# Second half of K in two 256-column banks, a new order of the queries, and memory reciprocals kept in PSUM

## The chip, the cores and the metric

The kernel runs on one core of a Trainium2 chip. The metric is the device time in microseconds (us) of one execution. The core has five engines with a queue each: TensorE (PE, with its weight loads shown apart as PEld), VectorE (DVE), ScalarE (ACT), GpSimd (POOL) and SyncE (SP, which here only issues DMAs). Matmuls write PSUM, eight banks of 512 fp32 columns; ScalarE and VectorE read it from there.

## The reference

Two things are computed from `x` (2048 rows of 512) and mixed by a gate. The part that matters is an attention that runs over 64 segments of 32 rows, one after the other, and hands eight memory rows from each to the next:

```python
for s in range(n_seg):                       # 64 segments of 32 rows
    h = jnp.concatenate([mem, xs], axis=1)   # 8 memory rows + 32 rows
    q, k, v = h @ Wq, h @ Wk, h @ Wv         # 32 heads of 128
    scores = jnp.einsum('bhqe,bhke->bhqk', q, k) * scale
    scores = jnp.where(mask[None, None], scores, -1000000000.0)
    p = _softmax(scores, axis=-1)
    o = jnp.einsum('bhqk,bhke->bhqe', p, v)
    o = jnp.einsum('bhte,hed->btd', o, Wo)
    mem = o[:, :M, :].copy()                 # the next segment needs this
    outs.append(o[:, M:, :])
...
return g * a + (1 - g) * b                   # a: attention, b: an MLP on x
```

The mask lets the eight memory queries see all keys and the others only earlier ones.

## The kernel before

It has three stages: the MLP (`b`) and the gate for all rows, the loop over the 64 segments, and a tail for the last segment. The order of the work on each engine is written out by hand; nothing is moved by a scheduler. Each engine takes its instructions in the order written, and waits are put in where data or buffers ask for them.

**How a segment is cut.** Of the 40 rows of a segment, 32 go through the step-by-step path: the eight memory rows and the first 24 others ("ride", `RIDE`). The last eight rows ("left", `LEFT`) don't hang on the memory, so their Q, K and V are made for four segments at once, ahead of time, as side work (`left_qk`, `left_v`), and so is their output projection (`wo_left`), behind time. The generator `fill` deals the side work out in units of four matmuls of 512 columns; `run(W1)`, `run(W2)` and `run(W3)` put two units each at three places of the segment, and what is left goes at the end.

**Order of a segment** (the `for s` loop; lines as in the profile):

1. Projections (`qk_unit`, L110): Q and K, each in two halves of 16 heads, into the four banks `U[0]` to `U[3]`, in the order Q0, K0, Q1, K1. A half is 16 matmuls of 512 columns: four chunks of the contraction, times four tiles of 32 array columns that run side by side. After each half ScalarE casts the bank to `Tb` (`qk_cast`, L115) and VectorE transposes it in 32x32 blocks into `QT` or `KT` (`qk_tr`, L119). After Q0 stand the four matmuls that write the mask into the second score bank (`mask_mm(1)`, L248).
2. First scores (`scores(s, 0)`, L256 and L260): heads 0 to 15 into bank `SbF`, on top of the mask, then two exps (L674): memory queries, then the rest.
3. V (`v_unit`, L129): the first half into bank `X1` (four groups), its cast (L689); one group of the second half into `X2`; the sums for the memory queries of the first heads (`msum(0)`, L267 and L270) and their normalising (`mnorm(0)`: reciprocal to `R`, L681, and multiply into `E`, L682); one more V group.
4. Second scores (`scores(s, 1)`): heads 16 to 31 into bank `W`, two exps, and a copy of the left queries' part of `E` into a zero-padded tile `EZ` (L699); the last two V groups and the cast of V's second half (L702); `msum(1)` and `mnorm(1)`.
5. `run(W1)`; the sums of the other queries (`xsums`, L605) and their reciprocal (`recip_x`, L616), which goes through DRAM to be spread over all partitions (`r_dr`, `Rb`, on SP); GpSimd adds the reciprocals to a running check (`racc`, L621).
6. Attention times V (`av`, L280 and L285): heads 0 to 15, then 16 to 31, into `U`; it needs both V casts and the normalised `E`.
7. ScalarE copies the memory columns to `UT` (L712) and the others to `XR` (`x_raw`, L611); `run(W2)`; output projection into `W` (`wo_pass`, L141), cast to `w` (L635); the mask for the first score bank; `run(W3)`; in every fourth segment the finished 128 rows of output are put together (`out_sel`, L226 and L228).
8. Selection of the memory rows (L724) and their cast into the next segment's input `hT` (L725), from which the next projections start.

GpSimd brings the other inputs to `hT` (`prep_h`, L239), the left queries to `QT` (`prep_q`, L243), and multiplies `XR` by `Rb` (`x_norm`, L629) during the next segment. The order of the columns of `QT`, and so of the scores and of `E`, is memory, ride, left. `E` has 56 columns per head: left keys with memory queries (0 to 8), all other keys with the 40 queries (8 to 48), left keys with left queries (48 to 56).

Of the kernel before, what the change touches and what calls it, by code (L numbers as in the profile page):

```python
# [27 lines left out]
def kernel(ctx, tc, A_x, A_mem0, A_Wq, A_Wk, A_Wv, A_Wo, A_seg_len, B_x, B_w1, B_b1, B_w2, B_b2, gate_w, out):  # L28
# [78 lines left out]
    def qk_unit(bk, G, t, hf, kc):  # L107
        h0, h1 = HF[hf]
        for j in range(4):
            nc.tensor.matmul(bk[32 * j:32 * j + 32, :], lhsT=G[:, kc, :], rhs=W5[t][:, kc, h0:h1, j, :],  # L110
                             start=(kc == 0), stop=(kc == KC - 1), tile_position=(0, 32 * j))

    def qk_cast(bk):
        Tb = ew.tile([P, 8, 32, 2], BF16, tag="Tb", bufs=3, name="Tb")
        nc.scalar.copy(out=Tb[:], in_=bk.rearrange("p (a b e) -> p a e b", a=8, b=2))  # L115
        return Tb

    def qk_tr(Tb, dst, hf):
        nc.vector.transpose(out=dst[:, 8 * hf:8 * hf + 8, 0:32, :].rearrange("p a r b -> p a (r b)").bitcast(FP32),  # L119
                            in_=Tb[:].rearrange("p a e b -> p (a e b)").bitcast(FP32))  # L120
# [115 lines left out]

    def prep_h(s):
        T, si = divmod(s, SPT)
        nc.gpsimd.tensor_copy(out=hT[s % 3][:, :, M:32], in_=xTs[T][:, :, seg * si:seg * si + RIDE])  # L239

    def prep_q(s):
        T, si = divmod(s, SPT)
        nc.gpsimd.tensor_copy(out=QT[:, :, 32:40, :].bitcast(FP32),  # L243
                              in_=QL[T % 2][:].bitcast(FP32).rearrange("p a (l s) b -> p a l s b", s=SPT)[:, :, :, si])

# [19 lines left out]
    def sums(out, E, c_main, c_left, n, start):  # L265
        for j in range(4):
            nc.tensor.matmul(out[32 * j:32 * j + 32], lhsT=BO[:, 32 * j:32 * j + 32], rhs=E[:, :, c_main:c_main + n],  # L267
                             start=start, stop=False, skip_group_check=True, tile_position=(0, 32 * j))
        for j in range(4):
            nc.tensor.matmul(out[32 * j:32 * j + 32, :, n - 8:n], lhsT=BO[:, 32 * j:32 * j + 32], rhs=E[:, :, c_left:c_left + 8],  # L270
                             start=False, stop=True, skip_group_check=True, tile_position=(0, 32 * j))
# [20 lines left out]
    with tc.tile_pool(name="mlpw", bufs=1) as mlpw, \  # L292
# [81 lines left out]
        for c in range(4):  # L374
            nc.gpsimd.affine_select(out=SelM[:], in_=SelM[:], pattern=[[-1, M]], compare_op=ALU.not_equal, fill=1.0, base=-32 * c, channel_multiplier=1)
            nc.gpsimd.affine_select(out=SelI[:], in_=SelI[:], pattern=[[-1, 32]], compare_op=ALU.not_equal, fill=1.0, base=-32 * c, channel_multiplier=1)
            nc.gpsimd.affine_select(out=SelR[:, 0:RIDE], in_=SelR[:, 0:RIDE], pattern=[[-1, RIDE]], compare_op=ALU.not_equal, fill=1.0, base=-32 * c - M, channel_multiplier=1)
            nc.gpsimd.affine_select(out=SelL[:].rearrange("p (s t) -> p s t", s=SPT)[:, :, RIDE:seg], in_=SelL[:].rearrange("p (s t) -> p s t", s=SPT)[:, :, RIDE:seg],
                                    pattern=[[-LEFT, SPT], [-1, LEFT]], compare_op=ALU.not_equal, fill=1.0, base=-32 * c, channel_multiplier=1)

        def consts():
            nc.vector.tensor_scalar(out=rr[:, 0:1], in0=ri[:], scalar1=31, scalar2=None, op0=ALU.bitwise_and)
            nc.vector.tensor_scalar(out=rr[:, 2:3], in0=rr[:, 0:1], scalar1=2, scalar2=None, op0=ALU.logical_shift_right)
            nc.vector.tensor_scalar(out=rr[:, 1:2], in0=rr[:, 0:1], scalar1=3, scalar2=None, op0=ALU.bitwise_and)
            nc.vector.tensor_copy(out=rf[:], in_=rr[:])
            nc.vector.tensor_copy(out=iof[:], in_=io[:])
            nc.vector.tensor_scalar(out=rf[:, 0:1], in0=rf[:, 0:1], scalar1=float(M), scalar2=None, op0=ALU.subtract)
            nc.vector.tensor_scalar(out=mk1[:], in0=iof[:, 0:4], scalar1=rf[:, 1:2], scalar2=MASK_NEG, op0=ALU.not_equal, op1=ALU.mult)
            yield
            for a in range(4):  # L390
                nc.vector.tensor_scalar(out=Mk[:, a, 16:16 + RIDE], in0=iof[:], scalar1=rf[:, 0:1], scalar2=MASK_NEG, op0=ALU.is_lt, op1=ALU.mult)
                nc.vector.tensor_copy(out=Mk[:, a, 0:8], in_=mk1[:, a:a + 1].to_broadcast([P, 8]))
                nc.vector.tensor_scalar(out=Mk[:, a, 48:56], in0=iof[:, 0:8], scalar1=rf[:, 2:3], scalar2=MASK_NEG, op0=ALU.is_lt, op1=ALU.mult)
                nc.vector.tensor_scalar(out=Mk[:, a, 48:56], in0=Mk[:, a, 48:56], scalar1=mk1[:, a:a + 1], scalar2=None, op0=ALU.add)
                yield
# [84 lines left out]
        def first():  # L480
# [3 lines left out]
            dve_q.append(lambda: nc.vector.tensor_copy(out=hT[0][:, :, 0:M], in_=m0p))  # L484
# [112 lines left out]
    EZ = [lp.tile([P, NG, 32], BF16, name=f"EZ{i}") for i in range(2)]  # L597
    for i in range(2):
        nc.gpsimd.memset(EZ[i][:, :, 0:RIDE], 0.0)

    def xsums(s, E):
        for first, src, c0 in ((True, E, 16), (False, EZ[s % 2], 0)):
            for i in range(NG):
                c, h = i % 4, i // 4
                nc.tensor.matmul(xs8[32 * c:32 * c + 32, 4 * h:4 * h + 4], lhsT=src[:, i, c0:c0 + 32], rhs=BO[:, 0:P:32],  # L605
                                 start=first and h == 0, stop=not first, skip_group_check=True, tile_position=(0, 32 * c))

    def x_raw(s):
        XR = cw.tile([P, 4, NG, 32], BF16, tag="XR", name="XR")
        for j in range(4):  # L610
            nc.scalar.copy(out=XR[:, j], in_=U[j][:, 0:NG * 40].rearrange("p (i q) -> p i q", q=40)[:, :, 8:40])  # L611
        XRs[s] = XR

    def recip_x(s):
# [5 lines left out]
        nc.sync.dma_start(Rb[:].rearrange("p r e -> p (r e)"), r_dr[s % 2][:].rearrange("r e -> (r e)").partition_broadcast(P))  # L620
        nc.gpsimd.tensor_tensor(out=racc[:, 0:RW], in0=racc[:, 0:RW], in1=R[:, 0:RW], op=ALU.add)  # L621
        Rbs[s] = Rb

    def x_norm(s):
        T, si = divmod(s, SPT)
        XR, Rb = XRs.pop(s), Rbs.pop(s)[:].rearrange("p (c q) (h j) -> p h j c q", c=4, h=2)
        for out, o, a, b in ((UT[(s + 1) % 2], M, 0, RIDE), (UL[T % 2], LEFT * si, RIDE, 32)):
# [10 lines left out]
    W1, W2, W3 = 2, 2, 2  # L638
    for s in range(nseg):
        T, si = divmod(s, SPT)  # L640
        last = s == nseg - 1
        hc, hn = hT[s % 3], hT[(s + 1) % 3]
        fill = side(T, si)
# [13 lines left out]
        for n, (t, hf) in enumerate(((0, 0), (1, 0), (0, 1), (1, 1))):  # L657
# [14 lines left out]
        def exps(i2, x):  # L672
            c = slice(16, EW) if x else slice(0, 16)
            nc.scalar.activation(out=E[:, 4 * i2:4 * i2 + 4, c], in_=Sb[i2][:, :, c], func=ACTF.Exp, scale=scale)  # L674

        def msum(i2):
            sums(U[i2][:, 320:352].rearrange("p (i q) -> p i q", q=8), E[:, 4 * i2:4 * i2 + 4, :], 8, 0, 8, True)
# [27 lines left out]
        msum(1)  # L705
        mnorm(1)
# [4 lines left out]
        for j in (0, 2, 1, 3):  # L711
            nc.scalar.copy(out=UT[s % 2][:, j, :, 0:M], in_=U[j][:, 0:NG * 40].rearrange("p (i q) -> p i q", q=40)[:, :, 0:8])  # L712
# [12 lines left out]
        nc.vector.tensor_copy(out=hn[:, :, 0:M], in_=W[:, 0:KC * M].rearrange("p (k m) -> p k m", k=KC))  # L725
# [8 lines left out]
    sums(xsum, E, 16, 48, 32, True)  # L734
# [6 lines left out]
    nc.vector.tensor_tensor(out=E[:, :, 16:48], in0=E[:, :, 16:48], in1=Rr, op=ALU.mult)  # L741
    nc.vector.tensor_tensor(out=E[:, :, 48:56], in0=E[:, :, 48:56], in1=Rr[:, :, 24:32], op=ALU.mult)
    av(s, V, E)
    UF = UT[(s + 1) % 2]
    for j in (0, 2, 1, 3):
        (nc.scalar.copy if j % 2 == 0 else nc.vector.tensor_copy)(out=UF[:, j], in_=U[j][:, 0:NG * 40].rearrange("p (i q) -> p i q", q=40)[:, :, 8:40])
# [147 lines left out]
```

## Time and profile before

| | us |
|---|---|
| median of 3 runs | 795.08 (794.21 to 796.0) |
| the profiled execution | 796.19 |
| its span, first to last instruction | 794.4 |
| loop over segments starts (first Q projection) | 98.7 |
| a segment, from one first Q projection to the next (median) | 10.65; every fourth 10.85 |
| last segment's first Q projection | 774.5 |
| mean granted TensorE clock | 0.998 |

The loop is 676 us of 794. TensorE is busy 97% of the span, ScalarE 68%, VectorE 41%, GpSimd 35%. The matmuls of a group overlap, so TensorE's 97% does not say that it works at its peak; the waits are to be read from when groups start. In the timeline a row gives start and length in us, engine, line, operation and the tiles written and read; a number in brackets is the idle time of the engine ahead of it and what ended it.

### The profile page before, as it was taken

The numbers are of one execution on the slowest core, as the hardware profiler recorded it, in microseconds if no ns is written. First come the engines' busy times: TensorE is split into PE (matmuls) and PEld (weight loads), VectorE is DVE, ScalarE is ACT, GpSimd is POOL, SyncE is SP. The second block draws the span as 40 slices with busy tenths as digits, with TensorE's granted clock in tenths as the row PEclk, the third lists the DMA queues.
The fourth block names the chain that finished last, engine by engine and source line by source line (L and its number), as shares of the span: only waits on it lengthen the run. The fifth ranks groups of instructions, "written<-read, shape, count | busy, mean of one in ns | idle before, by whom it ended". The sixth has DMA issues, their size and how long they took to land.

```text
span 794.4 us, 42412 instructions
## 1 busy us (share of the span) xinstructions
PE 767.9 (97%) x18921; PEld 428.8 (54%) x18950; DVE 327.7 (41%) x1061; ACT 539.9 (68%) x1503; POOL 277.8 (35%) x519
## 2 busy tenths in 40 slices
PE   7999999999999999999999999999999999999996
PEld 5666555555555555555555555555555555555553
DVE  4776344333334343434343333434343434333334
ACT  3666676766777676767776677777677767776663
POOL 3111033343344434234334324443334434332332
PEclk9999999999999999999999999999999999999999
DMA  6779411212111222211121212122221212121211
GB/s 189 265 269 350 142 59 58 74 60 86 60 53 68 77 70 70 77 57 60 60 86 61 86 61 75 46 75 70 78 70 57 62 58 86 61 80 60 71 65 36
DMA packets 46723, 70.49 MB, mean 89 GB/s; under 512 B 12799, under 2 KB 36456, under 8 KB 45000
## 3 DMA queue, kind: packets, MB, share of 16 engines
q1 hardware_dynamic: 45016, 64.97, 25.0%
q8 instruction: 150, 2.46, 1.3%
q0 software_dynamic: 720, 1.97, 0.7%
q10 hardware_dynamic: 800, 0.79, 0.3%
q14 instruction: 37, 0.30, 0.1%
HBM read 59.06 MB, written 4.45 MB: 80 GB/s over the span
## 4 chain that ended last, share of the span: by engine, by line
PE 93%; ACT 4%; issue 1%; DVE 1%; DMA 1%; POOL 0%; SPq 0%; DVEq 0%; POOLq 0%; ACTq 0%
PE U L110 28%; PE X L129 18%; PE W L141 14%; PE X L110 7%; PE U L468 5%; PE U L280 4%; PE X L141 3%; ACT w L635 3%; PE W L462 3%; PE SbF L462 3%; PE W L724 2%; PE U L267 1%; PE SbF L605 1%; PE SbF L256 1%; PE W L248 1%
## 5 line engine op out<-in xcount | busy, mean ns | idle before, releaser
L629 POOL TENSOR_TENSOR UT<-XR,Rb 128x384 bf16<-128x384 bf16 x126 | 140.0, 1132 | 271.8 <-DMA Rb<-r_dr 211.7
L115 ACT CAST Tb<-U 128x512 bf16<-128x512 f32 x258 | 151.0, 585 | 83.2 <-PE U L110 82.7
L110 PEld LDWEIGHTS <-hT 128*32 128x32 bf16 x4096 | 103.9, 97 | 109.7 <-DVE hT L725 19.1
L110 PE MATMUL U<-Wq_sb,hT 128*32 128x512 bf16 x2048 | 132.8, 379 | 1.1 <-DVE hT L725 1.1
L129 PE MATMUL X<-Wv_sb,hT 128*32 128x512 bf16 x2048 | 133.2, 378 | 0.0
L110 PE MATMUL U<-Wk_sb,hT 128*32 128x512 bf16 x2048 | 132.7, 379 | 0.0
L141 PE MATMUL W<-Wo_sb,UT 128*32 128x512 bf16 x2080 | 124.6, 380 | 1.5 <-ACT UT L712 1.2
L725 DVE CAST hT<-W 128x32 bf16<-128x32 f32 x63 | 12.1, 192 | 231.2 <-PE W L724 231.2
L119 DVE STREAM_TRANSPOSE QT<-Tb 128x256 f32<-128x256 f32 x128 | 57.0, 445 | 82.2 <-ACT Tb L115 81.1
L141 PEld LDWEIGHTS <-UT 128*32 128x32 bf16 x2080 | 57.2, 96 | 58.0 <-POOL racc L621 19.0
L119 DVE STREAM_TRANSPOSE KT<-Tb 128x256 f32<-128x256 f32 x128 | 57.0, 445 | 58.2 <-ACT Tb L115 58.2
L611 ACT CAST XR<-U 128x256 bf16<-128x256 f32 x252 | 78.6, 438 | 0.0
L635 ACT CAST w<-W 128x512 bf16<-128x512 f32 x65 | 38.0, 585 | 45.2 <-PE W L141 45.2
L629 POOL TENSOR_TENSOR UL<-XR,Rb 128x128 bf16<-128x128 bf16 x126 | 60.4, 500 | 0.0
L712 ACT CAST UT<-U 128x64 bf16<-128x64 f32 x252 | 35.3, 227 | 31.3 <-PE U L285 31.3
L129 PEld LDWEIGHTS <-hT 128*32 128x32 bf16 x2048 | 45.2, 95 | 20.7
L681 DVE RECIPROCAL R<-U 128x32 f32<-128x32 f32 x126 | 45.0, 357 | 25.9 <-PE U L270 23.0
L621 POOL TENSOR_TENSOR racc<-racc,R 128x72 f32<-128x72 f32 x63 | 21.2, 336 | 97.9 <-DVE R L616 95.2
L468 PE MATMUL U<-w_sb,hTm 128*128 128x512 bf16 (+1 forms) x163 | 49.5, 381 | 0.6
L115 ACT CAST Tb<-X 128x512 bf16<-128x512 f32 x62 | 36.5, 589 | 16.4 <-PE X L110 16.4
L462 PEld LDWEIGHTS <-w_sb 128*128 128x128 bf16 (+1 forms) x352 | 34.7, 102 | 21.1 <-issue 4.0
L256 PEld LDWEIGHTS <-KT 128*32 128x32 bf16 x2048 | 33.7, 95 | 16.3 <-DVE KT L119 0.2
(158 smaller groups left out, 1176.0 us busy)
## 6 DMA issues: line engine op xcount, KB each, us to landing
Rb<-r_dr SPq DMA_DIRECT2D x63, 512.0 KB, 3.9
Wv_sb<-in_A_Wv_dram SPq DMA_DIRECT2D x4, 1024.0 KB, 7.0
Wq_sb<-in_A_Wq_dram SPq DMA_DIRECT2D x4, 1024.0 KB, 7.2
Wk_sb<-in_A_Wk_dram SPq DMA_DIRECT2D x4, 1024.0 KB, 10.7
Wo_sb<-in_A_Wo_dram SPq DMA_DIRECT2D x4, 1024.0 KB, 14.8
VP<-VL SPq DMA_DIRECT2D x64, 64.0 KB, 3.0
xt<-in_A_x_dram SPq DMA_DIRECT2D x16, 128.0 KB, 2.7
xs<-in_A_x_dram SPq DMA_DIRECT2D x16, 128.0 KB, 2.3
```

The source lines that it names most:

```text
L110: nc.tensor.matmul(bk[32 * j:32 * j + 32, :], lhsT=G[:, kc, :], rhs=W5[t][:, kc, h0:h1, j, :], start=(kc == 0), stop=(kc == KC - 1), tile_ ...
L115: nc.scalar.copy(out=Tb[:], in_=bk.rearrange("p (a b e) -> p a e b", a=8, b=2))
L119: nc.vector.transpose(out=dst[:, 8 * hf:8 * hf + 8, 0:32, :].rearrange("p a r b -> p a (r b)").bitcast(FP32), in_=Tb[:].rearrange("p a e b ...
L129: nc.tensor.matmul(bk[32 * j:32 * j + 32, :], lhsT=G[:, kc, :], rhs=Wv5[:, kc, 4 * vb:4 * vb + 4, j, :], start=(kc == 0), stop=(kc == KC - ...
L141: nc.tensor.matmul(bk[32 * c:32 * c + 32, :], lhsT=U_[:, j, i, :], rhs=Wo_sb[:, 4 * i + j, :], start=(n == 0), stop=(n == NW - 1), tile_po ...
L256: nc.tensor.matmul(Sb[i2][32 * j:32 * j + 32, i - 4 * i2, M:M + 40], lhsT=KT[:, h // 2, :, h % 2], rhs=QT[:, h // 2, :, h % 2], start=Fals ...
L462: nc.tensor.matmul(hp[:rows, 0:TB * P], lhsT=w1_sb[:, kc, fc * P:fc * P + rows], rhs=yTs[blk][:, kc, :], start=(kc == 0), stop=(kc == KC - 1))
L468: nc.tensor.matmul(bp(blk, tt)[:], lhsT=hTm[blk % 2][:rows, fc, tt * P:(tt + 1) * P], rhs=w2_sb[:rows, fc, :], start=(fc == 0), stop=(fc = ...
L611: nc.scalar.copy(out=XR[:, j], in_=U[j][:, 0:NG * 40].rearrange("p (i q) -> p i q", q=40)[:, :, 8:40])
L629: nc.gpsimd.tensor_tensor(out=out[:, :, 4 * h:4 * h + 4, o:o + b - a], in0=XR[:, :, 4 * h:4 * h + 4, a:b], in1=Rb[:, h, :, :, a:b], op=ALU ...
L635: nc.scalar.copy(out=w[:], in_=W[:])
L681: nc.vector.reciprocal(out=r, in_=U[i2][:, 320:352])
```

## The change

1. **Second half of K.** K1 is projected in two quarters of eight heads, 256 columns each: the first into `U[3]`, the second into `X2`. Each has its own cast and its own transpose (`k_tr`). Matmul instructions for K1 go from 16 to 32.
2. **Query order.** Left, ride, memory instead of memory, ride, left, in `hT`, `QT`, `E`, the masks, the selections and the copies out of `U`. Left and ride are then neighbours: `xsums` reads left queries straight from `E`, as eight columns, and the padded tile `EZ` and its copy are gone. In every segment's `E` the columns 0 to 40 are the other queries and 40 to 56 the memory queries.
3. **Order after the first scores.** `mask_mm(1)` stands behind the first scores instead of behind Q0. The first bank's two exps become one of 56 columns per head. The second scores come after three V groups instead of six, both memory sums after the second scores, and V ends behind them (three groups behind the second sums). Both V casts stand behind all exps.
4. **Memory reciprocals in PSUM.** `mnorm` writes its reciprocals to spare columns of the two score banks (`RP`) and multiplies from there; two copies in `recip_x` bring them to `R` later, for the check.
5. **Smaller ones.** `out_sel` does its last matmul, 128 array columns wide, as four tiles of 32. The side work is dealt out 1, 2, 3 instead of 2, 2, 2 in the second and third segment of each four.

```diff
     def qk_unit(bk, G, t, hf, kc):
-        h0, h1 = HF[hf]
+        h0, h1 = hf if isinstance(hf, tuple) else HF[hf]
...
     def qk_cast(bk):
         Tb = ew.tile([P, 8, 32, 2], BF16, tag="Tb", bufs=3, name="Tb")
-        nc.scalar.copy(out=Tb[:], in_=bk.rearrange("p (a b e) -> p a e b", a=8, b=2))
+        n = bk.shape[1] // 64
+        nc.scalar.copy(out=Tb[:, 0:n], in_=bk.rearrange("p (a b e) -> p a e b", a=n, b=2))
         return Tb
+    def k_tr(Tb, a0, n):
+        nc.vector.transpose(out=KT[:, a0:a0 + n].rearrange("p a r b -> p a (r b)").bitcast(FP32),
+                            in_=Tb[:, 0:n].rearrange("p a e b -> p (a e b)").bitcast(FP32))
...
-        nc.tensor.matmul(bk[:], lhsT=SelL[:], rhs=wls.pop(T)[:], start=False, stop=True, skip_group_check=True)
+        wl = wls.pop(T)
+        for si in range(SPT):
+            nc.tensor.matmul(bk[32 * si:32 * si + 32, :], lhsT=SelL[:, 32 * si:32 * si + 32], rhs=wl[:], start=False, stop=True,
+                             skip_group_check=True, tile_position=(0, 32 * si))
...
+    RP = [bk[:, 288:320] for bk in (SbF, W)]
...
-        for first, src, c0 in ((True, E, 16), (False, EZ[s % 2], 0)):
+        for first, c0, n in ((True, 8, 32), (False, 0, LEFT)):
             for i in range(NG):
                 c, h = i % 4, i // 4
-                nc.tensor.matmul(xs8[32 * c:32 * c + 32, 4 * h:4 * h + 4], lhsT=src[:, i, c0:c0 + 32], rhs=BO[:, 0:P:32],
+                nc.tensor.matmul(xs8[32 * c:32 * c + n, 4 * h:4 * h + 4], lhsT=E[:, i, c0:c0 + n], rhs=BO[:, 0:P:32],
...
+        for i2 in (1, 0):
+            nc.vector.tensor_copy(out=R[:, 32 * i2:32 * i2 + 32], in_=RP[i2])
         nc.gpsimd.tensor_tensor(out=racc[:, 0:RW], in0=racc[:, 0:RW], in1=R[:, 0:RW], op=ALU.add)
...
-    W1, W2, W3 = 2, 2, 2
+    WS = ((2, 2, 2), (1, 2, 3), (1, 2, 3), (2, 2, 2))
...
-        for n, (t, hf) in enumerate(((0, 0), (1, 0), (0, 1), (1, 1))):
+        for n, (t, hf) in enumerate(((0, 0), (1, 0), (0, 1))):
...
             if n == 0:
                 flush(act_q, 9)
-                mask_mm(1)
                 flush(dve_q, 9)
-            qk_tr(qk_cast(bk[:]), (QT, KT)[t], hf)
+            qk_tr(qk_cast(bk[:]), (QT, KT)[t], hf, LEFT * (1 - t))
+        for bk, a0 in ((U[3], NP // 2), (X2, 3 * NP // 4)):
+            n = NP // 4
+            bk = bk[:, 0:64 * n]
+            for kc in range(KC):
+                qk_unit(bk, hc, 1, (2 * a0, 2 * a0 + 2 * n), kc)
+            k_tr(qk_cast(bk), a0, n)
...
         def mnorm(i2):
-            r, e = R[:, 32 * i2:32 * i2 + 32], E[:, 4 * i2:4 * i2 + 4, 0:16].rearrange("p i (a q) -> p i a q", q=8)
+            r, e = RP[i2], E[:, 4 * i2:4 * i2 + 4, 40:56].rearrange("p i (a q) -> p i a q", q=8)
...
         scores(s, 0)
-        for i2 in range(2):
-            exps(0, i2)
-        for kc in range(KC):
+        mask_mm(1)
+        nc.scalar.activation(out=E[:, 0:4, :], in_=Sb[0], func=ACTF.Exp, scale=scale)
+        for kc in range(3):
             v_unit(X1, hc, 0, kc)
-        nc.scalar.copy(out=v_out(V, 0), in_=X1[:])
-        v_unit(X2, hc, 1, 0)
-        if not last:
-            msum(0)
-            mnorm(0)
-        v_unit(X2, hc, 1, 1)
         scores(s, 1)
         for i2 in range(2):
             exps(1, i2)
         if not last:
-            nc.scalar.copy(out=EZ[s % 2][:, :, RIDE:32], in_=E[:, :, 48:56])
-        for kc in range(2, KC):
+            msum(0)
+            mnorm(0)
+        v_unit(X1, hc, 0, 3)
+        nc.scalar.copy(out=v_out(V, 0), in_=X1[:])
+        v_unit(X2, hc, 1, 0)
+        if not last:
+            msum(1)
+            mnorm(1)
+        for kc in range(1, KC):
             v_unit(X2, hc, 1, kc)
         nc.scalar.copy(out=v_out(V, 1), in_=X2[:])
         if last:
             break
-        msum(1)
-        mnorm(1)
         run(W1)
```

The rest of the diff renumbers columns and slices for the new query order, in the masks, the selections and the tail.

More of the change, by code (lines that the diff above doesn't have):

```diff
@@ L269, in sums @@
         for j in range(4):
-            nc.tensor.matmul(out[32 * j:32 * j + 32, :, n - 8:n], lhsT=BO[:, 32 * j:32 * j + 32], rhs=E[:, :, c_left:c_left + 8],
+            nc.tensor.matmul(out[32 * j:32 * j + 32, :, 0:8], lhsT=BO[:, 32 * j:32 * j + 32], rhs=E[:, :, c_left:c_left + 8],
                              start=False, stop=True, skip_group_check=True, tile_position=(0, 32 * j))
@@ L375 @@
             nc.gpsimd.affine_select(out=SelM[:], in_=SelM[:], pattern=[[-1, M]], compare_op=ALU.not_equal, fill=1.0, base=-32 * c, channel_multiplier=1)
-            nc.gpsimd.affine_select(out=SelI[:], in_=SelI[:], pattern=[[-1, 32]], compare_op=ALU.not_equal, fill=1.0, base=-32 * c, channel_multiplier=1)
+            for q0, a, b in ((0, RIDE, 32), (LEFT, 0, RIDE)):
+                nc.gpsimd.affine_select(out=SelI[:, a:b], in_=SelI[:, a:b], pattern=[[-1, b - a]], compare_op=ALU.not_equal, fill=1.0, base=-32 * c - q0, channel_multiplier=1)
             nc.gpsimd.affine_select(out=SelR[:, 0:RIDE], in_=SelR[:, 0:RIDE], pattern=[[-1, RIDE]], compare_op=ALU.not_equal, fill=1.0, base=-32 * c - M, channel_multiplier=1)
@@ L483, in first @@
                 nc.tensor.transpose(m0p[:, kc, :], m0[:, kc * P:(kc + 1) * P], ident[:M, :M])
-            dve_q.append(lambda: nc.vector.tensor_copy(out=hT[0][:, :, 0:M], in_=m0p))
+            dve_q.append(lambda: nc.vector.tensor_copy(out=hT[0][:, :, RIDE:32], in_=m0p))
             yield from x_mm(0, X2)
@@ L610, in x_raw @@
         for j in range(4):
-            nc.scalar.copy(out=XR[:, j], in_=U[j][:, 0:NG * 40].rearrange("p (i q) -> p i q", q=40)[:, :, 8:40])
+            nc.scalar.copy(out=XR[:, j], in_=U[j][:, 0:NG * 40].rearrange("p (i q) -> p i q", q=40)[:, :, 0:32])
         XRs[s] = XR
@@ L626, in x_norm @@
         XR, Rb = XRs.pop(s), Rbs.pop(s)[:].rearrange("p (c q) (h j) -> p h j c q", c=4, h=2)
-        for out, o, a, b in ((UT[(s + 1) % 2], M, 0, RIDE), (UL[T % 2], LEFT * si, RIDE, 32)):
+        for out, o, a, b in ((UT[(s + 1) % 2], M, LEFT, 32), (UL[T % 2], LEFT * si, 0, LEFT)):
             for h in range(2):
@@ L642 @@
         hc, hn = hT[s % 3], hT[(s + 1) % 3]
+        W1, W2, W3 = WS[si]
         fill = side(T, si)
@@ L711 @@
         for j in (0, 2, 1, 3):
-            nc.scalar.copy(out=UT[s % 2][:, j, :, 0:M], in_=U[j][:, 0:NG * 40].rearrange("p (i q) -> p i q", q=40)[:, :, 0:8])
+            nc.scalar.copy(out=UT[s % 2][:, j, :, 0:M], in_=U[j][:, 0:NG * 40].rearrange("p (i q) -> p i q", q=40)[:, :, 32:40])
         x_raw(s)
@@ L724 @@
             nc.tensor.matmul(W[:, M * k:M * k + M], lhsT=w[:, k * P:(k + 1) * P], rhs=SelM[:], start=(k == 0), stop=(k == KC - 1), skip_group_check=True)
-        nc.vector.tensor_copy(out=hn[:, :, 0:M], in_=W[:, 0:KC * M].rearrange("p (k m) -> p k m", k=KC))
+        nc.vector.tensor_copy(out=hn[:, :, RIDE:32], in_=W[:, 0:KC * M].rearrange("p (k m) -> p k m", k=KC))
         flush(dve_q, 9)
@@ L733 @@
     nx = slice(8 * NG, 40 * NG)
-    sums(xsum, E, 16, 48, 32, True)
+    sums(xsum, E, 8, 0, 32, True)
     for _ in out_sel(T - 1, X2):
@@ L740 @@
     Rr = R[:, nx].rearrange("p (i q) -> p i q", q=32)
-    nc.vector.tensor_tensor(out=E[:, :, 16:48], in0=E[:, :, 16:48], in1=Rr, op=ALU.mult)
-    nc.vector.tensor_tensor(out=E[:, :, 48:56], in0=E[:, :, 48:56], in1=Rr[:, :, 24:32], op=ALU.mult)
+    nc.vector.tensor_tensor(out=E[:, :, 8:40], in0=E[:, :, 8:40], in1=Rr, op=ALU.mult)
+    nc.vector.tensor_tensor(out=E[:, :, 0:8], in0=E[:, :, 0:8], in1=Rr[:, :, 0:8], op=ALU.mult)
     av(s, V, E)
@@ L745 @@
     for j in (0, 2, 1, 3):
-        (nc.scalar.copy if j % 2 == 0 else nc.vector.tensor_copy)(out=UF[:, j], in_=U[j][:, 0:NG * 40].rearrange("p (i q) -> p i q", q=40)[:, :, 8:40])
+        (nc.scalar.copy if j % 2 == 0 else nc.vector.tensor_copy)(out=UF[:, j], in_=U[j][:, 0:NG * 40].rearrange("p (i q) -> p i q", q=40)[:, :, 0:32])
     flush(dve_q, 9)
```

24 lines of the change are left out of this document (11 added, 13 removed).

## The prediction

> **What bounds the kernel now.** I read the page's busy times first, then the timeline of one segment, then that of a segment near the end that has no side work, and last the groups of instructions with their shapes kept apart.
>
> ```profile
> span 794.4 us, 42412 instructions
> ...
> PE 767.9 (97%) x18921; PEld 428.8 (54%) x18950; DVE 327.7 (41%) x1061; ACT 539.9 (68%) x1503; POOL 277.8 (35%) x519
> ```
>
> TensorE looks full, but that row counts overlapping matmuls. The segment that starts near 399.4 us shows what its stretches wait for (columns: start, length, engine, line, operation, what ended the idle time).
>
> ```profile
> 402.99 0.27 PE L256 MATMUL SbF<-QT,KT 128*32 128x40 bf16 x16
> ...
> 403.12 1.25 PE L129 MATMUL X<-Wv_sb,hT 128*32 128x512 bf16 x20
> ...
> 403.21 0.58 ACT L115 CAST Tb<-U 128x512 bf16<-128x512 f32 x1 [0.28 <-PE U L110]
> ...
> 403.83 0.45 DVE L119 STREAM_TRANSPOSE KT<-Tb 128x256 f32<-128x256 f32 x1 [0.42 <-ACT Tb L115]
> ...
> 404.47 0.27 PE L256 MATMUL W<-QT,KT 128*32 128x40 bf16 x16
> ...
> 404.60 0.61 PE L129 MATMUL X<-Wv_sb,hT 128*32 128x512 bf16 x8
> 404.82 0.10 PEld L267 LDWEIGHTS <-BO 128*32 128x32 bf16 x1
> 404.86 0.42 ACT L674 ACTIVATE E<-W 128x64 bf16<-128x64 f32 x2
> ...
> 405.13 0.20 PE L267 MATMUL U<-E,BO 128*32 128x32 bf16 x4
> ...
> 405.46 0.58 ACT L702 CAST V<-X 128x512 bf16<-128x512 f32 x1
> ...
> 405.88 0.23 DVE L682 TENSOR_TENSOR E<-E,R 128x64 bf16<-128x64 bf16 x1
> ...
> 406.15 0.28 PE L280 MATMUL U<-E,V 32*128 32x40 bf16 x16
> ...
> 406.87 1.91 PE L141 MATMUL W<-Wo_sb,UT 128*32 128x512 bf16 x32
> ```
>
> The reader should see: the last K matmuls end shortly after 402.99; their cast and transpose end at 404.28, just before the second scores at 404.47. The second sums (405.13) come 0.53 after those scores end (404.60), though only 0.43 of V work lies between. The second half of attention times V (406.15) starts 0.05 after the multiply on VectorE ends (405.88 + 0.23). So from the second scores on it is a chain of hand-overs that sets the time, and the side work fills its holes. The proof is a segment that has no side work:
>
> ```profile
> 762.36 0.28 PE L248 MATMUL SbF<-Mk,ident 128*32 128x224 bf16 x4
> 762.59 0.58 ACT L635 CAST w<-W 128x512 bf16<-128x512 f32 x1 [0.65 <-PE W L141]
> 763.23 0.26 PE L724 MATMUL W<-SelM,w 128*128 128x8 bf16 x4 [0.59 <-ACT w L635]
> ```
>
> Its first projections start at 753.17 and the next segment's at 763.84, 10.67 apart; a segment with eight units of side work takes 10.70 (410.29 to 420.99). A fill that is moved is therefore worth nothing as long as it ends inside the wait it fills. The rows also price one hand-over: from the end of the output projection's issue (762.36) over a 512-wide cast to the next matmul (763.23) it is 0.87.
>
> **The change part by part**, counted from the start of the first scores (0 = 402.99), per segment; there are 63 whole ones.
>
> *Ahead of the scores.* The mask matmuls of the second score bank leave the projections: four matmuls take 0.095 (411.16 to 411.25, next group's start). The second half of K becomes 32 matmuls of 256 columns. A group of four 512-wide ones takes 0.216 (20 matmuls, five groups, 403.12 to 404.20), the 224-wide mask group 0.095, so a 256-wide group takes 0.108 and eight take 0.87, against 0.86: +0.01. Together -0.085.
>
> *Up to the second scores.* First scores 0.13, mask 0.095, three V groups 0.65: TensorE is there at 0.87, and after the half that needs the third quarter of K, at 0.925. The last quarter of K isn't there yet. Its cast starts at 0.22, as now (403.21). Then come a 256-wide cast, a hand-over of 0.04 (402.35 + 0.58 to 402.97), a 128-wide transpose and 0.07 from a VectorE write to the matmul that reads it (410.03 + 0.19 to 410.29). Neither width stands alone in the trace. The nearest rows:
>
> ```profile
> L611 ACT CAST XR<-U 128x256 bf16<-128x256 f32 x252 | 78.6, 438 | 0.0
> ...
> L712 ACT CAST UT<-U 128x64 bf16<-128x64 f32 x252 | 35.3, 227 | 31.3 <-PE U L285 31.3
> ...
> L125 DVE STREAM_TRANSPOSE KL<-Tb 128x128 f32<-128x128 f32 x64 | 20.4, 397 | 7.8 <-ACT Tb L115 7.8
> ```
>
> Cast: by the line through 64 columns (0.227) and 512 (0.585) it is 0.38; the 256-wide copies (0.438) run four in a row, overlapping; half of 0.585, 0.29, is the low end. I take 0.38. Transpose: two KL ones are 0.21 apart (0.61 for two of 0.397), and a 256-wide one lets the next start after 0.36 (410.94 to 411.30), so 128 columns less save about 0.14 of 0.445: 0.31. High end 0.397 (that one scatters its output; this one doesn't), low end half of 0.445, 0.22. I take 0.31. Ready at 0.22 + 0.38 + 0.04 + 0.31 + 0.07 = 1.02: a new stall of about 0.10 (0 by the low ends, which give 0.84; 0.24 by the high ends, 1.165). What stands behind the waiting matmul is all of TensorE's work.
>
> *From there to the second half of attention times V.* The rest of the second scores, 0.08, ends at 1.10. The first sums (0.055) and two V groups (0.43) end at 1.59; the second sums need the second scores' first exp, 0.53 after those as now, so 1.63: stall 0.05 (0 if part of the 0.53 is the V cast of 404.21 that ScalarE still finishes at 404.79). Sums and the last three V groups end at 2.34. Now V is last where it was early: its cast and hand-over are the 0.87 above, less a little as this cast takes 0.578: 0.86, so 3.20. Now it is 406.15 - 402.99 = 3.16. Net: +0.04.
>
> *Costed at nothing, and what hides it.* The normalising chain on VectorE (sums, 0.36, 0.23 twice) ends near 2.7, half a microsecond before V's cast; reading its factor from another memory could cost 0.3 more without showing. ScalarE loses the padded copy (0.24), one exp call, and gains about 0.06 for a split cast: in the rows the copy stands right ahead of V's cast, but V is late now for TensorE's sake. The two copies of reciprocals to R (0.19 each, by the 128x32 cast L725) end before the output projection, which overwrites their bank, 0.71 after the second V half starts; without that cover each would cost 0.19. GpSimd's accumulation waits for them, and behind it the left queries and the next inputs; GpSimd idles 5.92 before its next product (413.19), waiting for the broadcast, and no DMA is issued from behind the copies (both issues stand ahead). The side work moves by one unit (0.216) in two of four segments: before the V half at most 0.43 + 0.10 + 0.10 + 0.15 lies under 0.86, and after the output projection 0.095 + 0.65 + 0.10 under 0.87. The output selection does four tiles for one full matmul, 0.216 either way, 14 times; a change of array shape (0.10, what L285 at 406.26 takes beyond its 0.03 until L110 starts at 406.39) moves by one place; one more or less would be 1.4 us in all. Mask constants, identities and fills that are gone lie in the first 98 us, beside TensorE's mixer work. The last segment lengthens by about 0.1 in all.
>
> Sum: -0.085 + 0.04 = about -0.05 per segment (-0.049 before rounding), times 63 = **-3.1 us**. The profiled execution took 796.19 with a span of 794.4, so its span would be 791.3. The median of the three runs shown is 1.11 below that execution: 795.08 - 3.1 = **792.0**.
>
> **The rivals.**
>
> *The K hand-over is slow (slower).* With the burst cast (0.438) and the KL transpose (0.397) the last quarter is ready at 1.165, the stall is 0.24, and the segment grows by 0.09: +5.8, **800.8**. It decides from a ready time of 1.07 on. For: these are the only rows of these widths, and nothing hides the stall. Against: both rows are from instructions that run back to back.
>
> *No stall at all (faster).* By the low ends the last quarter is there in time: -0.15 per segment, -9.4, **785.7**; with the exp early too, -0.20, 782.6. For: the exp finds ScalarE idle. Against: halving a width halves no row here (0.227 for 64 columns against 0.585 for 512).
>
> *Side work is throughput (faster).* If TensorE's 97% were real, the third unit behind the output projection would fill 0.216 of idle time in 32 segments, 6.9 more: **785.1**. Against: the segment without side work takes as long as one with it.
>
> *Weight loads come out from behind the narrower matmuls (slower).* A set of four loads lasts 0.11 (the mask's at 410.94); if each of the four additional sets showed, +0.44 per segment, 28 us, **820**. Against: 20 score matmuls, each with its own load, take 0.13, and 512-wide groups show no load at all. The Trainium skill ("TensorE: Matmul & The Clock Gate", Part 3, the mechanism) says that a load overlaps running matmuls only where the row groups differ, which here they don't; with its 27 ns for 32 columns (Part 2, same page) the 16 additional loads would cost 0.43 per segment by estimate. The trace disagrees: four such loads beside 512 columns would make 0.32 per group, and the row says 0.216.
>
> That the edits end up elsewhere than written can be left out: the order is by hand, and the changed program's instruction order has the second scores wait on VectorE in two places.
>
> **How the numbers follow.** About 0.2% (1.6 us) is what a measurement here can tell from no change. My forecast, a stall of 0.05 to 0.15, has 0.53: from 789 to 795.1, of it 0.40 below 793.5 and 0.13 within 0.2%. Slow K hand-over 0.26, no stall 0.13, side work 0.05, weight loads 0.03. So faster 0.40 + 0.13 + 0.05 = 0.58, same 0.13, slower 0.29. The range, 785 to 801, reaches the no-stall case and the slow hand-over; the forecast's own is 789 to 795.
>
> **What would show it.** Right: the second scores start 0.87 after the first and break for about 0.1 in the middle; the half-width KT transpose takes about 0.31 and its cast 0.38; the second V half starts 0.05 after V's cast ends, not after the multiply; output projection to selection stays 0.87. Wrong: a break over 0.15 there, 256-wide groups above 0.12, output projection or selection starting later after what feeds them, or a GpSimd or VectorE row ending the wait before them.

## The result, and the profile after

| | before | changed |
|---|---|---|
| median, us | 795.28 (6 runs, 794.21 to 796.0) | 791.27 (6 runs, 790.55 to 792.25) |
| ratio to before, 95% interval | | 0.9949 (0.9939 to 0.9958) |
| span of the profiled execution | 794.4 | 789.8 |
| a segment, median | 10.65; every fourth 10.85 | 10.57; every fourth 10.77 |
| from first Q projection to first scores | 3.55 | 3.46 |
| from first scores to second half of attention times V | 3.16 | 3.16 |

Repeated beside later experiments, the changed kernel had a ratio of 0.9936 (0.9924 to 0.9949). So the change makes the kernel faster by 4 to 5 us. The page's first lines for the changed kernel:

```profile
span 789.8 us, 45014 instructions
...
PE 767.8 (97%) x20019; PEld 454.0 (57%) x20019; DVE 337.4 (43%) x1252; ACT 522.2 (66%) x1440; POOL 278.8 (35%) x521
```

The span is 4.6 shorter, and these rows don't say why. The page of before has 18,950 weight loads but only 18,921 matmuls, so 29 matmul records are missing there, and its 767.9 us of TensorE can't be set against the 767.8 here; by the weight loads, one to a matmul, the changed kernel issues 1,069 more. ScalarE has 17.7 us less to do, almost four times what the span lost. Where the gain lies is read from the stretches of a segment. One segment in the timeline (columns as before):

```profile
401.22 0.27 PE L267 MATMUL SbF<-QT,KT 128*32 128x40 bf16 x16
...
401.36 0.27 PE L259 MATMUL W<-Mk,ident 128*32 128x224 bf16 x4
...
401.45 0.37 ACT L116 CAST Tb<-X 128x256 bf16<-128x256 f32 x1
401.45 0.82 PE L134 MATMUL X<-Wv_sb,hT 128*32 128x512 bf16 x12
...
401.62 0.54 DVE L120 STREAM_TRANSPOSE KT<-Tb 128x128 f32<-128x128 f32 x2
...
401.94 0.40 PEld L267 LDWEIGHTS <-KT 128*32 128x32 bf16 x16 [0.17 <-DVE KT L120]
402.10 0.35 PE L267 MATMUL W<-QT,KT 128*32 128x40 bf16 x16
...
402.54 0.42 ACT L696 ACTIVATE E<-W 128x64 bf16<-128x64 f32 x2 [0.46 <-PE U L281]
...
402.82 0.20 PE L278 MATMUL U<-E,BO 128*32 128x32 bf16 x4
...
403.64 0.22 DVE L704 TENSOR_TENSOR E<-E,W 128x64 bf16<-128x64 bf16 x1
...
403.75 0.59 ACT L725 CAST V<-X 128x512 bf16<-128x512 f32 x1 [0.31 <-PE X L134]
...
404.39 0.27 PE L291 MATMUL U<-E,V 32*128 32x40 bf16 x16
```

Read it against the rows of before. The second scores start 0.88 after the first (402.10 against 401.22) instead of 1.48, and spread over 0.35 where they took 0.27: the break in their middle. The transposes of the two quarters (L120) stand in one row; the weight loads' 0.17 is the wait for the first. The second ends at 402.16, and inside the merged row of loads the next set starts at 402.22, 0.05 behind it, after 0.085 without a new matmul. The second half of attention times V (404.39) starts 0.05 after V's cast ends (403.75 + 0.59) and 0.53 after the multiply ends (403.64 + 0.22): the last wait of this stretch has changed hands, from VectorE to ScalarE. The new rows of the two widths that the trace of before did not have, from the groups with shapes kept apart (last numbers: busy us, mean ns):

```profile
L120 DVE STREAM_TRANSPOSE KT<-Tb 128x128 f32<-128x128 f32 x128 | 35.4, 291 | 0.0
...
L116 ACT CAST Tb<-U 128x256 bf16<-128x256 f32 x64 | 24.2, 378 | 0.0
```

The 291 is a mean over both quarters: the third quarter of K takes 0.270, the last 0.311.

### The profile page after: what moved, and what is told of

Its sections match the earlier page's. It is cut to its first block, busy times and chain, and to the rows that moved or that the text cites. A ratio compares the mean times of both kernels' runs of the same rounds, so it can differ in the third digit from the quotient of the medians.

```text
span 789.8 us, 45014 instructions
## 1 busy us (share of the span) xinstructions
PE 767.8 (97%) x20019; PEld 454.0 (57%) x20019; DVE 337.4 (43%) x1252; ACT 522.2 (66%) x1440; POOL 278.8 (35%) x521
## 4 chain that ended last, share of the span: by engine, by line
PE 95%; DVE 2%; ACT 1%; DMA 1%; issue 1%; POOL 0%; DVEq 0%; SPq 0%; ACTq 0%; POOLq 0%
PE U L110 25%; PE X L134 18%; PE W L146 14%; PE X L110 11%; PE U L482 5%; PE X L146 4%; PE U L291 3%; PE W L476 3%; PE SbF L476 3%; PE W L267 1%; PE W L745 1%; PE SbF L617 1%; DVE R L628 1%; PE SbF L267 1%; PE W L259 1%; PE SbF L259 1%
## 5 line engine op out<-in xcount | busy, mean ns | idle before, releaser
L110 PEld LDWEIGHTS <-hT 128*32 128x32 bf16 x5120 | 131.7, 97 | 104.2 <-DVE hT L746 19.5
L116 ACT CAST Tb<-U 128x512 bf16<-128x512 f32 (+1 forms) x258 | 131.3, 535 | 60.9 <-PE U L110 60.4
L134 PE MATMUL X<-Wv_sb,hT 128*32 128x512 bf16 x2048 | 137.9, 377 | 0.0
L110 PE MATMUL U<-Wk_sb,hT 128*32 128x512 bf16 (+1 forms) x2048 | 105.4, 326 | 0.0
L116 ACT CAST Tb<-X 128x256 bf16<-128x256 f32 (+1 forms) x126 | 60.3, 479 | 18.1 <-PE X L110 18.1
L482 PE MATMUL U<-w_sb,hTm 128*128 128x512 bf16 (+1 forms) x176 | 52.9, 385 | 0.0
L134 PEld LDWEIGHTS <-hT 128*32 128x32 bf16 x2048 | 44.9, 94 | 13.4
L725 ACT CAST V<-X 128x512 bf16<-128x512 f32 x64 | 37.5, 586 | 19.6 <-PE X L134 19.6
L267 PEld LDWEIGHTS <-KT 128*32 128x32 bf16 x2048 | 38.2, 95 | 15.1 <-DVE KT L120 8.7
L696 ACT ACTIVATE E<-W 128x64 bf16<-128x64 f32 (+1 forms) x128 | 26.8, 261 | 29.3 <-PE U L281 28.7
```

Of the source, the lines that this page charges most:

```text
L116: nc.scalar.copy(out=Tb[:, 0:n], in_=bk.rearrange("p (a b e) -> p a e b", a=n, b=2))
L267: nc.tensor.matmul(Sb[i2][32 * j:32 * j + 32, i - 4 * i2, M:M + 40], lhsT=KT[:, h // 2, :, h % 2], rhs=QT[:, h // 2, :, h % 2], start=Fals ...
L482: nc.tensor.matmul(bp(blk, tt)[:], lhsT=hTm[blk % 2][:rows, fc, tt * P:(tt + 1) * P], rhs=w2_sb[:rows, fc, :], start=(fc == 0), stop=(fc = ...
L725: nc.scalar.copy(out=v_out(V, 1), in_=X2[:])
```

## The experiments

Unless said otherwise, an edit is made to the changed kernel, whose time to compare with is 791.3 (ratio 0.995).

### The second half of K, whole again

```diff
-        for n, (t, hf) in enumerate(((0, 0), (1, 0), (0, 1))):
+        for n, (t, hf) in enumerate(((0, 0), (1, 0), (0, 1), (1, 1))):
...
-        for bk, a0 in ((U[3], NP // 2), (X2, 3 * NP // 4)):
...
-            k_tr(qk_cast(bk), a0, n)
```

> The changed kernel with the second half of K whole again: one bank of 512 columns, one cast, one transpose; all else as changed. Theory (the chain of hand-overs sets the time): last K matmuls end 0.17 after the first scores start, cast from 0.22 for 0.585, hand-over 0.04, transpose 0.445, 0.07 to the matmul: ready at 1.35, where the changed kernel's second scores start at 0.87 and end at 1.09. All of the second scores wait, so they end at 1.48: +0.39 per segment, -0.01 for wider matmuls, times 63 = +24 us on 791.3: about 815, slower than before the change. Rival (the split buys nothing, since before the change the transpose ended in time): the narrower groups' 0.01 comes back, 790.6. The second scores' wait in the trace tells them apart.

Measured: 815.2 us, ratio 1.0241 (1.0221 to 1.0261). The timeline of this kernel:

```profile
410.10 0.27 PE L267 MATMUL SbF<-QT,KT 128*32 128x40 bf16 x16
...
410.33 0.58 ACT L116 CAST Tb<-U 128x512 bf16<-128x512 f32 x1 [0.22 <-PE U L110]
...
410.94 0.45 DVE L124 STREAM_TRANSPOSE KT<-Tb 128x256 f32<-128x256 f32 x1 [0.36 <-ACT Tb L116]
...
411.44 0.28 PE L267 MATMUL W<-QT,KT 128*32 128x40 bf16 x16 [0.30 <-DVE KT L124]
```

The cast starts 0.23 after the first scores, as with the split, and the second scores 1.34 after them, waiting for the transpose. The earlier second scores are affordable only with the split: all the rest of the change without it costs 19 us against the kernel before (796.4 in the same series).

### The second mask back in its old place

```diff
                 flush(act_q, 9)
+                mask_mm(1)
                 flush(dve_q, 9)
...
         scores(s, 0)
-        mask_mm(1)
```

> The changed kernel with the second mask back behind the first projection. Theory: behind the first scores the mask lies under the wait for the last quarter of K (ready at 1.01 after the first scores start, whatever TensorE does meanwhile); taken away from there it leaves a wait of 0.18 in place of 0.086, and ahead of the scores it costs its 0.095: +6.0 us, 797.3. Rival (the mask is TensorE work on the path in either place): 791.3, unchanged.

Measured: 796.9 us, ratio 1.0013 (1.0003 to 1.0023): the whole gain is gone. The stretch to the first scores grows from 3.46 to 3.56, and the one from there to the second half of attention times V stays at 3.16. In the timeline the second scores start earlier (0.77 after the first) and break for longer:

```profile
414.41 0.27 PE L267 MATMUL SbF<-QT,KT 128*32 128x40 bf16 x16
...
414.79 0.56 DVE L120 STREAM_TRANSPOSE KT<-Tb 128x128 f32<-128x128 f32 x2
...
415.11 0.41 PEld L267 LDWEIGHTS <-KT 128*32 128x32 bf16 x16 [0.25 <-DVE KT L120]
415.18 0.45 PE L267 MATMUL W<-QT,KT 128*32 128x40 bf16 x16
```

0.45 instead of 0.35: the mask's 0.095 has become waiting.

### The mask moved, alone

This edit is made to the kernel before, with the same two lines the other way round.

```diff
                 flush(act_q, 9)
-                mask_mm(1)
                 flush(dve_q, 9)
...
         scores(s, 0)
+        mask_mm(1)
```

> The kernel before with only the second mask moved behind the first scores, as in the change. Theory: there is no wait under it there (the last K transpose ends 0.19 before the second scores, six V groups after the first), so it delays the second scores by the 0.095 that it saves ahead of the first: no change, ratio 1.000 to the kernel before. Rival (taking the mask out of the projections is the gain in itself): -0.095 per segment, -6.0 us, ratio 0.9925.

Measured: 796.7 us, ratio 1.0006 (0.9997 to 1.0016), no change. The first stretch falls to 3.45 and the second grows to 3.26. Together with the run above: the mask is worth its 0.095 only where it lies under a wait, and that wait comes with the earlier second scores.

### Side work dealt 2, 2, 2

```diff
-    WS = ((2, 2, 2), (1, 2, 3), (1, 2, 3), (2, 2, 2))
+    WS = ((2, 2, 2),) * 4
```

> The changed kernel with the side work dealt 2, 2, 2 in all segments. Theory: both places end in a wait that is longer than the work in it (0.87 from the last V group to the second half of attention times V, 0.87 from output projection to selection), so 791.3 within 0.1%. Rival (TensorE throughput counts): one unit of 0.216 fewer behind the output projection in 32 segments, +6.9, 798.2; or, if it frees the V stretch, -6.9.

Measured: 791.6 us, ratio 0.994 (0.9923 to 0.9958). The median segment is 10.57, as with 1, 2, 3. Side work that moves inside the waits has no price.

### The two small parts undone, together and one by one

Together:

```diff
         def mnorm(i2):
-            r, e = RP[i2], E[...]
+            r, e = R[:, 32 * i2:32 * i2 + 32], E[...]
...
-        for i2 in (1, 0):
-            nc.vector.tensor_copy(out=R[:, 32 * i2:32 * i2 + 32], in_=RP[i2])
...
-        wl = wls.pop(T)
-        for si in range(SPT):
-            nc.tensor.matmul(bk[32 * si:32 * si + 32, :], lhsT=SelL[:, 32 * si:32 * si + 32], ...)
+        nc.tensor.matmul(bk[:], lhsT=SelL[:], rhs=wls.pop(T)[:], start=False, stop=True, skip_group_check=True)
```

> The changed kernel with memory reciprocals in R in SBUF as before (no copies from PSUM) and the output selection's last matmul whole again. Theory: the normalising chain ends about half a microsecond before V's cast, so where its factor lies costs nothing, and four tiles take as long as one matmul: the changed kernel's time, ratio 0.995. Rival (keeping them in PSUM is what helps, by keeping VectorE off GpSimd's memory, where the multiply took 0.54 in place of 0.23 in some segments): up to 0.3 per segment in the segments where both meet, ratio 0.998 or more.

Measured: 792.9 us, ratio 0.9964 (0.9951 to 0.9977), between the two forecasts. So the changed kernel and each half of this edit (the first two hunks, and the last) ran once more, on one chip:

> The changed kernel itself, beside the three below on one chip. Both theories: ratio 0.995 to the kernel before; it is the yardstick for the others.

> The changed kernel with the memory reciprocals in R in SBUF as before, alone. Theory (the normalising chain has half a microsecond to spare): the yardstick's time within 0.1%, median segment 10.57. Rival (PSUM keeps the multiply out of GpSimd's way and that counts): the 1.2 us by which the kernel with both small parts undone stood above the changed one are its, 0.15% slower, and the trace shows segments in which the second half of attention times V waits for the multiply.

> The changed kernel with the output selection's last matmul whole again, alone. Theory: 0.216 either way, so the yardstick's time within 0.1%. Rival (a second change of array shape costs 0.1 in each of 14 segments): 1.4 us slower, and the stretch from output projection to next projections longer than 1.71 in every fourth segment.

Measured: the changed kernel 791.8, ratio 0.9936 (0.9924 to 0.9949); reciprocals in SBUF 793.4, 0.9964 (0.9952 to 0.9976); selection whole 793.1, 0.9964 (0.9949 to 0.9978). Both stand above the yardstick by 1.2 to 1.6 us, and so does the kernel with both undone, so the two costs don't add up. The median segments are 10.57 and 10.77 in all four to within 0.003, and the stretch from output projection to the next projections is 1.706 in every fourth segment either way, so the rival of the selection does not show.

The rival of the reciprocals does, in a few segments. With them in SBUF, 19 of 126 multiplies take more than 0.3 us, up to 0.59, and all 19 run beside a GpSimd instruction; with them in PSUM none takes more than 0.224, though 27 in the changed kernel's first profile run beside GpSimd too. In four segments the second half of attention times V then starts 0.05 after such a multiply and not after V's cast. That comes to 0.3 us in the profile, not 1.6.

The expectation that these parts cost nothing in the median segment holds; that the time stays is not borne out, and where the rest lies is open. The profiles can't tell it: the profiled executions of the three took 793.03, 792.76 and 793.04, and the changed kernel's was its slowest.

### One V group more ahead of the second scores

```diff
-        for kc in range(3):
+        for kc in range(KC):
             v_unit(X1, hc, 0, kc)
         scores(s, 1)
-        for i2 in range(2):
-            exps(1, i2)
+        exps(1, 0)
+        nc.scalar.copy(out=v_out(V, 0), in_=X1[:])
+        exps(1, 1)
         if not last:
             msum(0)
             mnorm(0)
-        v_unit(X1, hc, 0, 3)
-        nc.scalar.copy(out=v_out(V, 0), in_=X1[:])
-        v_unit(X2, hc, 1, 0)
+        for kc in range(2):
+            v_unit(X2, hc, 1, kc)
         if not last:
             msum(1)
             mnorm(1)
-        for kc in range(1, KC):
+        for kc in range(2, KC):
             v_unit(X2, hc, 1, kc)
```

> The changed kernel with one more V group ahead of the second scores (four, then two, then two, in place of three, two, three), and the first V cast between the second half's two exps. Theory: the fourth group covers the wait for the last quarter of K (0.086, TensorE there at 1.09 and K at 1.01), V ends 0.086 earlier, and the second half of attention times V, which hangs on V's cast alone, with it: -0.083 per segment, -5.2, 786.0. Rival (the stall goes to another hand-over: the second sums, which wait for the exp, or the normalising chain, 1.02 from the second sums): 791.3, or slower if the V cast holds up the second exp.

Measured: 790.4 us, ratio 0.9923 (0.9903 to 0.9942). The break in the second scores is gone, as expected, and the median segment falls by 0.054, not 0.083. The missing 0.03 is at the second sums, in this kernel's timeline:

```profile
413.17 0.28 PE L267 MATMUL W<-QT,KT 128*32 128x40 bf16 x16
...
413.56 0.22 ACT L696 ACTIVATE E<-W 128x64 bf16<-128x64 f32 x1 [0.62 <-PE U L281]
...
413.84 0.20 PE L278 MATMUL U<-E,BO 128*32 128x32 bf16 x4
...
414.55 0.58 ACT L725 CAST V<-X 128x512 bf16<-128x512 f32 x1
...
414.91 0.22 DVE L704 TENSOR_TENSOR E<-E,W 128x64 bf16<-128x64 bf16 x1
...
415.19 0.27 PE L291 MATMUL U<-E,V 32*128 32x40 bf16 x16
```

From the second scores' end to the second sums it is 0.534 here and 0.505 in the changed kernel: the exp starts 0.276 after the last score matmul starts, against 0.248 there. So a part of the saved stall did go to the next hand-over. The normalising chain, the rival's other candidate, has lost its cover as well: the multiply and V's cast end together at 415.13, 0.06 ahead of the second half of attention times V. The profiled execution shows more breaks too (its segments sum to 4.0 more than their medians, against 1.4 and 3.1 in two of the changed kernel), so the time moved less than the median segment.

### One V group more, and both masks behind the output projection

```diff
-    Sb = [bk[:, 0:4 * EW].rearrange("p (i c) -> p i c", c=EW) for bk in (SbF, W)]
+    Sb = [SbF[:, 4 * EW * i:4 * EW * i + 4 * EW].rearrange("p (i c) -> p i c", c=EW) for i in range(2)]
...
-    xs8 = SbF[:, 256:256 + NG]
+    xs8 = SbF[:, 448:448 + NG]
...
-    RP = [bk[:, 288:320] for bk in (SbF, W)]
+    RP = [W[:, 288 + 32 * i:320 + 32 * i] for i in range(2)]
...
         scores(s, 0)
-        mask_mm(1)
...
         mask_mm(0)
+        mask_mm(1)
         run(W3)
```

In `mask_mm` only the first mask keeps `start=True`, and one call more stands ahead of the loop.

> The one-more-V-group kernel, side work 2, 2, 2, with both halves' scores side by side in one bank, so that both masks are written in the wait behind the output projection and none between the scores; the reciprocals lie in the other bank. Theory: with four V groups the wait for the last quarter of K is gone, so the mask between the scores is on the path again; without it the second scores start at 0.995 in place of 1.09, the last quarter being ready at 1.01: -0.095 in the segments that have a wait behind the output projection (47), none in every fourth, which is full there: -4.5, 785.9, ratio 0.987. Rival (the mask is hidden between the scores as it was in the changed kernel): 790.4.

> The kernel with four V groups ahead of the second scores and both score halves in one bank, again, for its distance to the changed kernel on one chip. Theory: median segments 10.42 in two of four, 10.51 and 10.72 in the others, against 10.57 and 10.77: 0.42% ahead of the yardstick in sum, 3.3 us, less what irregular breaks in the matmul stream take. Rival (its 788.6 was chance): no difference from the yardstick.

Measured: 788.6 us, ratio 0.9916 (0.9893 to 0.9938), and again 788.5, ratio 0.990 (0.9885 to 0.9914), beside 791.8 for the changed kernel: 3.3 us ahead of it. It is the fastest of all. The stretch from first scores to second V half falls to 3.02, and the median segments are 10.42, 10.42, 10.52 and 10.72. The gain is 0.095 in two segments of four, not three: in the last of each four the stretch behind the output projection, 0.88 before, grew to 0.98, so it was full as well, with the transposes of the next inputs. That leaves 3.0 us of the 4.5 expected; the time is 1.8 below that of the one-more-V-group kernel, which ran on another chip.

### One V group more, and the output projection in two halves

```diff
     def wo_pass(U_):
-        for n in range(NW):
-            wo_group(W, U_, n)
         w = cw.tile([P, Dm], BF16, tag="w", bufs=8, name="w")
-        nc.scalar.copy(out=w[:], in_=W[:])
+        for h, bk in enumerate((W, U[0])):
+            for n in range(NW):
+                wo_half(bk, U_, n, h)
+            nc.scalar.copy(out=w[:, 256 * h:256 * h + 256], in_=bk[:, 0:256])
         return w
```

`wo_half` is `wo_group` on 256 of the 512 columns.

> The one-more-V-group kernel (790.4), side work 2, 2, 2, with the output projection in two halves of 256 columns in two banks, each with its own cast. Theory (the last cast of a stage is a hand-over on the path, and half as wide it is 0.2 shorter): from output projection to selection 0.67 in place of 0.87 in the second and third segment of each four, which hold only 0.63 of work there; the first and fourth are full there (1.08 and 0.88) and gain next to nothing; the projection itself grows by 0.02. About 32 times 0.19 less 63 times 0.02: -5, 785.5, ratio 0.987. Rival (width of the hand-over doesn't matter, or weight loads show in 16 more groups of 256 columns): no change or slower, 790.4 to 797.

Measured: 805.3 us, ratio 1.0113 (1.0094 to 1.0132), slower. The hand-over did shrink as expected, from 0.874 to 0.647 in the second and third segment, and where no break falls such a segment takes 10.30, against 10.51 with the projection in one. The projection itself grew from 1.72 to 1.74, so weight loads don't show. What came in its place is in the view of waits of TensorE (us in all, times, longest):

```profile
PE U L291 <- issue: 5.8, 11, 0.8
PE X L110 <- issue: 1.9, 4, 0.7
PE W L649 <- issue: 1.8, 5, 0.6
```

"issue" is idle time in which the engine waits for nothing that the profile shows; over the same window the changed kernel's view has none of it, and the one-more-V-group kernel's 0.8 us. The breaks fall in the middle of a run of like matmuls:

```profile
432.42 0.19 PE L296 MATMUL U<-E,VP 32*128 32x64 bf16 x4
432.55 0.19 PE L291 MATMUL U<-E,V 32*128 32x40 bf16 x2
433.51 0.27 PE L291 MATMUL U<-E,V 32*128 32x40 bf16 x14 [0.78 <-issue]
```

Two of sixteen matmuls start, then nothing for 0.78. Counted against the segments without a break (10.74, 10.30, 10.30 and 10.53), 37 of the 63 are more than 0.1 longer, and together they lose 25 us; in the changed kernel, counted in the same way, 6 are in its first profile and 15 in its second.

## Why the prediction was right

**The sum.** Predicted was -0.05 per segment and -3.1 us; the median segment fell by 0.082, which is 5.2 us over 63, and the median time by 4.0. The span of the profiled execution fell by 4.6: there the loop starts 0.66 later (99.40 against 98.74) and its first segment takes 11.26 against 10.69. The start is not the change's: it lies between 97.95 and 99.40 in six profiles of the changed kernel and of its near copies. The first segment is long (10.81 to 11.80) in all the profiles of reordered kernels; in the changed kernel's its first sums wait 0.52 for the second half's exps (104.64), which in later segments they don't, and why is not shown. So that the time came within 0.8 of the 792.0 is in part luck: the usual segment gained 2.1 us more in all than forecast, and part of that went where the forecast had nothing.

**Ahead of the scores.** Predicted -0.085; measured 3.549 to 3.463, -0.086. A 256-wide group takes 0.109 (eight in 0.873), so weight loads did not come out. By a sentence of the Trainium skill ("TensorE: Matmul & The Clock Gate", Part 3, "The mechanism") a load overlaps running matmuls only where row groups differ; with the 27 ns of Part 2 of that page this gives 0.43 more per segment by estimate, and the trace disagrees here as it did before. The same section also lets a load run ahead into a background weight buffer, which would fit the row; no run here shows which of the two holds.

**The K hand-over.** Predicted 0.38 for the cast, 0.31 for the transpose, ready at 1.02, a stall of 0.10. Measured for the last quarter: 0.373, 0.311, ready at 1.00 (the matmul starts 0.054 after the transpose, where 0.07 was taken), a stall of 0.086. The middle values were right, but not for the reason given against the high ends, that those rows are from instructions that run back to back: the new cast starts 0.03 before the one ahead of it ends, the new transpose 0.025, and they take 0.373 and 0.311 all the same. What makes the rows of 0.438 and 0.397 longer is not shown, so the choice between far ends was in part luck. That this hand-over decides is shown from both sides: whole again it costs 24 us, with the mask out of its cover some 5.5, and with a fourth V group its stall is gone.

**From there on.** Predicted 3.20 to the second half of attention times V, measured 3.163. The mis-sized terms are the stall at the second sums (0.05 predicted, 0.018 measured, because the exp starts sooner after scores that were broken by a wait) and 0.015 of the K stall. V's cast as the last wait, with 0.86: the second sums to the second V half take 1.569, predicted 0.055 + 0.65 + 0.86 = 1.565. Both dealings of side work give that same 1.569, and the run with 2, 2, 2 confirms it.

**Costed at nothing.** The exps, the padded copy, the fills and the projection-to-selection stretch (0.874 to 0.875) are as predicted. For the reciprocals and the selection the median segment agrees and the time doesn't quite: 1.2 to 1.6 us when either is undone, of which the trace shows 0.3 for the reciprocals. In the changed kernel the multiply ends 0.53 ahead of the second V half, the half microsecond of the forecast.

**The rivals.** Slow K hand-over: ruled out by its rows. No stall at all: the stall stands in the trace. Side work as throughput: ruled out by the fill run, 791.6 where 798.2 or 784.4 was to be seen. Weight loads: above.

## What to carry to other kernels

In a chain of hand-overs, price a reorder by the ready time of what the moved step waits for, not by the work that it moves: the same mask matmuls were worth some 5.5 us under a wait, and nothing where no wait was. A split of a hand-over pays when its last piece is what the next step waits for, as long as the added instructions bring no breaks of their own (the split output projection); find what fills the wait that remains (a fourth group of V, then both masks elsewhere: 788.5). And check a segment without side work first: where it takes as long as one with it, moving side work is no lever.

## What was not expected

**The end of many small matmuls.** With 20 score matmuls in one run, the exp that reads them starts 0.276 after the last one starts (before, and with the fourth V group, where ScalarE had been idle for 0.62); with a wait right ahead of the run 0.264 (K whole); broken by a wait in the middle 0.248. The rows of the matmuls show no difference, so a run of small matmuls without a break seems to finish later than its rows say.

**Breaks without a releaser.** They grew with TensorE's rows in the kernel with the projection split (22,099 matmuls against 20,019), and beside them went the queue q8 of kind "instruction" on the page's list, from 158 packets to 175. The trace says more: each of the 32 "issue" breaks of that kernel between 105 and 770 us (0.16 to 0.78, 13.9 in all) ends 2.2 to 3.0 us after a packet of q8 starts, while the packets come some 4.0 us apart (median) and breaks at random would fall anywhere in that time. The three breaks of the one-more-V-group kernel fall at 2.3 to 2.7. That speaks for instruction supply as the cause; no run tested it.
